# A changed order between attention and the expert blocks: first weights, token rows, ranks and conversions

## The chip, the cores and the metric

One NeuronCore of a Trainium2 chip runs the whole kernel. The metric is the device time of one execution in microseconds (us), median of several runs. The engines are TensorE (PE; its weight loads are PEld), VectorE (DVE), ScalarE (ACT), GpSimd (POOL) and SyncE (SP), which only issues transfers here. Each engine works off its own instructions in order.

## The reference

Three parts follow each other on 2304 tokens of 512 features.

```python
# attention: 4 batches x 8 heads x 576 x 64, window of 128, a slope per head
scores = scale * q @ k.T - slope * rel            # only 0 <= rel < 128
x = softmax(scores) @ v                           # -> [2304, 512]
# top-1 mixture of 8 experts
logits = x @ w_gate + modality_bias[modality_id]
e = argmax(logits); p = softmax(logits)[e]
x = p * (relu(x @ w1[e]) @ w2[e])
# bilinear stage, weights given as 64-bit floats
out = ((x @ m_w1) * (x @ m_w2)) @ m_w3 @ m_wout
```

## The kernel before

**Numbers.** Float32 products are made of three passes: each operand is split into a high half (rounded to the type that TensorE takes, `fp32r`) and a low half (the rest), and `mm3` adds high x high, high x low and low x high. `split` makes the halves: ScalarE writes the high one (L264), VectorE subtracts for the low one (L266). 64-bit weights arrive as pairs of integers, and `to_f32` makes float32 of them in five VectorE instructions (L694, L698, L701, L704, L707), of which the last two write `x`.

**Stages.** (1) Attention in 40 units of two head pairs; 18 tiles of 128 tokens come out. Behind each tile `gate_logits` computes its logits and stores its rows to DRAM (`xz`). (2) For five groups of tiles `route` picks the expert of each token: one-hot rows `hot_b` (L531), running sums `hcum` (L536), two small matmuls that give the ranks `rk` (L540, L543), and from these the positions `pos1_i` (L556). GpSimd then scatters token numbers to `inv2`. (3) `block_table` starts from a matmul that counts the tokens (`cnt`, L574) and gives, in some 40 small VectorE instructions, for each block of 480 token slots its expert `eb_i`, its first row `row_i` (L630) and its first column. The first block has entries of its own (`eb0_i`, `row0_i`), which are there earlier. (4) The expert blocks: `gather_x` loads a block's token numbers (`ids`, on SP) and gathers its rows from `xz` in four groups of 120 (`xb`, indirect transfers that GpSimd issues); `block_transposes` turns a group round on TensorE (`btp`, four transposes) and splits it; `load_w` and `split_w` bring the expert's weights in eight steps per block (`fw`, halves `fwh` and `fwl`); `ffn_step` does the products (`ph`, `py`). (5) The last stage, `bilinear`, with weights `wt` and products `po` at its end.

**Beside attention.** Since the last two matrices are applied one after the other, m_w3 @ m_wout is computed in advance, in 64 steps (`w_step`, three matmuls of 512 columns each into `pw`, eight steps for one row of results, one bank for all, freed by the ScalarE copy at L759). m_w3 comes in 16 pieces of four steps each: `load_w3` loads one, `cvt_w3` converts it, `w3_transposes` transposes it (`w3tp`, four transposes) and splits it (`w3h`, `w3l`). The list `W_STEPS` says how many steps stand in each of the 40 attention units and the six places behind them: 40 steps in all, 34 of them inside the loop over units, six behind it. The last 24 steps (40 to 63, pieces 10 to 15) follow in a loop of their own, behind the table and the first loads. Steps are numbered from 0 and pieces too: piece 9 serves steps 36 to 39, piece 14 steps 56 to 59, piece 15 steps 60 to 63.

**Order.** The code is traced top to bottom, and a planner then orders each engine's instructions by the code's order and by the times that it expects. `high_priority(PRIO)` moves what it encloses forward in that order. `issue_after(ins)` is an edge: whatever the block issues on the engine of `ins` comes behind `ins` there; instructions of other engines are not touched by it. Before the change, only the last group's `route` has high priority, and it stands ahead of the six steps behind the loop.

**Behind w3's last piece.** `run_blocks` splits the first two weight steps behind the halves of piece 15, then transposes the first block's four row groups, then runs the steps, in which weights are split two steps and loaded three steps ahead.

**Memory.** Tiles live in pools, one stack from the left and one from the right of each partition. The pool of the expert blocks (`fp`: weights and, from another stage on, `wt`) lies on the left on top of the constants and a pad of `PAD` bytes, and the pool of the rows (`xp`) above it. Its lower part takes the place of the attention pool, so its first loads wait until that is free.

Of the kernel before, what the change touches and what calls it, by code (L numbers as in the profile page):

```python
# [18 lines left out]
P = 128  # L19
# [4 lines left out]
RU_LAST = 100  # L24
PAD = 32
NB_STATIC = 5
# [20 lines left out]
def kernel(  # L47
# [456 lines left out]
    def route(g, i0, m):  # L504
# [30 lines left out]
        for j in range(i0, i0 + m):  # L535
# [6 lines left out]
        )  # L542
        nc.tensor.matmul(  # L543
            rk[:, :m, :], lhsT=ones_b, rhs=hcum[:, sl, :], start=False, stop=True
# [10 lines left out]
        )  # L555
        nc.vector.tensor_tensor(out=pos1_i[:, sl], in0=mn, in1=rank[:, sl], op=ALU.add)  # L556
        for j in range(i0, i0 + m):
# [6 lines left out]
            tc.add_to_no_dep_group("scatter", sc.ins)  # L564

    def block_table():

# [4 lines left out]

        np_ = pst("A", [P, 6, E], "cnt")
        nc.tensor.matmul(np_[:, 0, :], lhsT=ones_b, rhs=hcum[:, NT, :], start=True, stop=True)  # L574

# [53 lines left out]
        nc.vector.tensor_scalar_mul(eb, eb, float(CAP))  # L629
        nc.vector.tensor_tensor(out=row_i, in0=r0, in1=eb, op=ALU.add)  # L630

# [50 lines left out]

    def to_f32(pool, raw_t, name, x=None):

# [5 lines left out]
        if x is None:  # L690
# [38 lines left out]

    def cvt_w3(i):  # L730
        st_w["x", i] = to_f32(w_p, st_w.pop(("3", i)), f"w3_{i}")

    def w3_transposes(i):
        x = st_w.pop(("x", i))
        h = w_p.tile([P, 4, P], F32R, tag="w3h", name=f"w3h_{i}", bufs=3)
        l = w_p.tile([P, 4, P], F32R, tag="w3l", name=f"w3l_{i}", bufs=3)
        tp = pst("A", [P, 4, P], f"w3tp_{i}")
        for j in range(4):
            nc.tensor.transpose(tp[:, j, :], x[:, j * P : (j + 1) * P], ident)
        split(h, l, tp)  # L740
        st_w["last"] = (last["a"], last["v"])
        st_w["T", i] = (h, l)
# [6 lines left out]
    def w_step(k):  # L749
# [6 lines left out]
        j = g % 4  # L756
        mm3(pw, h[:, j, :], l[:, j, :], woh[:, g, :], wol[:, g, :], g == 0, g == NG - 1)
        if g == NG - 1:
# [111 lines left out]
    for i in range(nu + 2):  # L870
# [36 lines left out]
    assert not w_jobs  # L907
# [86 lines left out]
    def block_transposes(b, u):  # L994
# [8 lines left out]
        for d in range(ND):  # L1003
            nc.tensor.transpose(tp[:, d, :ru], xb[b][u][:ru, d * P : (d + 1) * P], ident[:ru, :ru])
        us = slice(u * ru, (u + 1) * ru)
# [108 lines left out]
    def run_blocks(b0, b1, extra, after=()):  # L1114
        g0, g1 = b0 * NS, b1 * NS
        for g in range(g0, min(g0 + SA, g1)):
            with ExitStack() as st:
                for a in after:
                    st.enter_context(tc.issue_after(a.ins))
                split_w(g)  # L1120
        for u in range(NU):
            block_transposes(b0, u)
        for b in range(b0, b1):
            for s in range(NS):
                g = NS * b + s
                if g + LA < g1:
                    load_w(g + LA)
                if s == 0 and b + 1 < b1:
# [22 lines left out]
    x_p = xstk.enter_context(tc.tile_pool(name="xp", bufs=2))  # L1151
    first_loads(0, NB_STATIC)
# [363 lines left out]
    jobs.setdefault(g_mid + 1, []).append(lambda: load_wt(0, 1))  # L1516
    run_blocks(0, NB_STATIC, jobs, w3_last)
    with tc.tile_pool(name="cp", bufs=2) as c_p:
# [40 lines left out]
```

## Time and profile before

| | us |
|---|---|
| median of 3 runs | 760.69 |
| the three runs | 766.66, 760.69, 759.67 |
| profiled execution | 757.12 |
| its span, first to last instruction | 755.4 |
| TensorE busy | 734.9 |
| VectorE busy | 526.2 |
| ScalarE busy | 347.3 |
| GpSimd busy | 74.9 |

All rows come from the one profiled execution, in us from the start of its span. A row of instructions has its start, its duration, engine, line, operation, output and inputs, shape and count; in brackets stand the idle time just before it on this engine and what ended that. TensorE's matmuls are pipelined: one starts before the end of the last is reported, so the step from start to start is what counts.

### The profile page before, as it was taken

Reading aid. Unit: us, or ns where it says so; the run is one execution under the profiler, and the core shown is the slowest. Engines: PE = TensorE matmul, PEld = TensorE weight load, DVE = VectorE, ACT = ScalarE, POOL = GpSimd, SP = SyncE. Lnnn points to the kernel's source line nnn. Section 1 sums busy time; section 2 is a strip of 40 time slices with the busy share of each in tenths; the row PEclk is TensorE's granted clock in tenths of the full one; section 3 lists DMA queues with packets and bytes.
Section 4 is the critical chain, followed back from the end, with each engine's and each line's share of the span. In section 5 each row is a group of like instructions: output and inputs, shape, how many; then the busy total and the mean of one; then the engine's idle time right before and its main releaser. Section 6 shows DMA issues by size and latency. Waiting matters only on the chain. (4 is left out here: it accounts for less than half of the span.)

```text
span 755.4 us, 12359 instructions
## 1 busy us (share of the span) xinstructions
PE 734.9 (97%) x4335; PEld 631.5 (84%) x4335; DVE 526.2 (70%) x1351; ACT 347.3 (46%) x778; POOL 74.9 (10%) x105
## 2 busy tenths in 40 slices
PE   7899999999999999999999999999999999999996
PEld 5777777787877788888888899999789997899984
DVE  3688888767689469697994347888657775568721
ACT  4787775866842533333343438231632315323221
POOL 5000200201013202030020000000120001100011
PEclk9999999999999999999999999999999999999999
DMA  7999467264136947979698344643226432233011
GB/s 132 325 312 252 109 179 178 67 161 129 44 84 149 253 144 222 293 196 352 180 297 268 132 133 116 209 123 98 77 71 192 123 96 77 67 118 116 1 43 42
DMA packets 126416, 116.29 MB, mean 154 GB/s; under 512 B 69631, under 2 KB 100735, under 8 KB 126344
## 3 DMA queue, kind: packets, MB, share of 16 engines
q1 hardware_dynamic: 122664, 105.91, 48.7%
q0 software_dynamic: 3680, 9.49, 4.0%
q8 instruction: 36, 0.59, 0.4%
q14 instruction: 36, 0.29, 0.1%
HBM read 87.69 MB, written 27.51 MB: 153 GB/s over the span
## 5 line engine op out<-in xcount | busy, mean ns | idle before, releaser
L264 ACT ACTIVATE wth<-wt 128x896 fp32r<-128x896 f32 x48 | 43.0, 946 | 89.6 <-PE pP L1296 89.6
L266 DVE TENSOR_TENSOR fwl<-fw,fwh 128x1024 fp32r<-128x1024 f32 x40 | 48.8, 1225 | 46.3 <-ACT fwh L264 45.8
L397 ACT ACTIVATE p<-p,mn 128x256 f32<-128x256 f32 (+2 forms) x144 | 68.1, 475 | 21.3 <-DVE mn L392 21.0
L264 ACT ACTIVATE fwh<-fw 128x1024 fp32r<-128x1024 f32 x40 | 42.1, 1062 | 76.6 <-PE ph L282 58.9
L281 PE MATMUL ph<-xbh,fwh 128*128 128x480 f32 (+1 forms) x160 | 60.1, 376 | 0.7 <-ACT xbh L264 0.7
L282 PE MATMUL py<-Whl,fwh 128*128 128x480 f32 (+1 forms) x160 | 59.9, 375 | 0.0
L282 PE MATMUL ph<-xbl,fwh 128*128 128x480 f32 (+1 forms) x160 | 59.7, 373 | 0.0
L283 PE MATMUL ph<-xbh,fwl 128*128 128x480 f32 (+1 forms) x160 | 59.6, 373 | 0.0
L283 PE MATMUL py<-Whl,fwl 128*128 128x480 f32 (+1 forms) x160 | 57.8, 373 | 0.0
L281 PE MATMUL po<-Whl,abh 128*128 128x512 f32 x144 | 57.1, 397 | 0.6 <-ACT abh L264 0.6
L283 PE MATMUL po<-Whl,abl 128*128 128x512 f32 x144 | 57.1, 398 | 0.0
L281 PE MATMUL py<-Whl,fwh 128*128 128x480 f32 (+1 forms) x160 | 56.9, 373 | 0.0
L282 PE MATMUL po<-Whl,abh 128*128 128x512 f32 x144 | 56.8, 394 | 0.0
L266 DVE TENSOR_TENSOR abl<-ab,abh 128x512 fp32r<-128x512 f32 x36 | 24.7, 690 | 40.7 <-ACT abh L264 40.6
L266 DVE TENSOR_TENSOR wtl<-wt,wth 128x896 fp32r<-128x896 f32 x48 | 51.8, 1083 | 1.6 <-ACT wth L264 1.4
L392 DVE CUSTOM_DVE_ANT_0 p<-S,bias 128x256 f32<-128x256 f32 (+1 forms) x128 | 43.8, 385 | 12.6 <-PE S L366 12.2
L1305 DVE TENSOR_TENSOR c<-pA,u 128x384 f32<-128x384 f32 x48 | 26.7, 557 | 33.9 <-PE pA L1296 31.7
L264 ACT ACTIVATE abh<-ab 128x512 fp32r<-128x512 f32 x36 | 22.5, 630 | 57.6 <-PE po L282 40.2
L454 PE MATMUL av<-pT,vr 128*64 128x128 f32 (+2 forms) x576 | 47.9, 275 | 0.0
L1401 POOL DMA_INDIRECT out_dram<-o,sid x18 | 21.6, 1200 | 262.9 <-ACT o L1400 262.9
L454 PEld LDWEIGHTS av<-pT,vr 128*64 128x64 f32 (+1 forms) x576 | 32.5, 136 | 11.5 <-issue 5.0
L418 PE MATMUL PT<-ident,p 128*128 128x128 f32 x224 | 41.0, 290 | 0.3
(256 smaller groups left out, 1944.6 us busy)
## 6 DMA issues: line engine op xcount, KB each, us to landing
wt<-wT SPq DMA_DIRECT2D x48, 448.0 KB, 3.3
fw<-in_moe_w_dram SPq DMA_DIRECT2D x40, 512.0 KB, 4.2
raw_w<-in_moe_w_dram SPq DMA_DIRECT2D x16, 512.0 KB, 5.1
raw_m<-in_moe_w_dram SPq DMA_DIRECT2D x32, 256.0 KB, 5.4
wT<-ms SPq DMA_DIRECT2D x16, 448.0 KB, 5.4
yT<-zf SPq DMA_DIRECT2D x20, 256.0 KB, 5.8
x<-yT SPq DMA_DIRECT2D x12, 384.0 KB, 5.5
vr<-in_v_dram SPq DMA_DIRECT2D x16, 256.0 KB, 4.6
```

Of the source, the lines that this page charges most:

```text
L264: last["a"] = nc.scalar.activation(out=hi, in_=src, func=AF.Copy, scale=scale)
L266: last["v"] = nc.vector.tensor_tensor(out=lo, in0=src, in1=f32(hi), op=ALU.subtract)
L281: nc.tensor.matmul(dst, lhsT=lh, rhs=rh, start=start, stop=False)
L282: nc.tensor.matmul(dst, lhsT=lh, rhs=rl, start=False, stop=False)
L283: return nc.tensor.matmul(dst, lhsT=ll, rhs=rh, start=False, stop=stop)
L392: nc.vector.tensor_tensor_reduce(out=p[:, j, t, :nk], in0=s[j][:, t, :nk], in1=bi, scale=1.0, scalar=BIG, op0=ALU.add, op1=ALU.min, accum_ ...
L397: nc.scalar.activation(out=p[:, j, t, :nk], in_=p[:, j, t, :nk], func=AF.Exp, scale=-1.0, bias=m1, accum_out=sm[:, col : col + 1],)
L418: nc.tensor.transpose(pt[:, t, kb, :], p[:, j, t, kb * P : (kb + 1) * P], ident)
L454: nc.tensor.matmul(av[j * D : (j + 1) * D, hp, cs], lhsT=raw["v", b, cc][:n_k, 2 * hp + j, :], rhs=rhs, start=(i_k == 0), stop=(i_k == len ...
L1305: last["d"] = nc.vector.tensor_tensor(out=out, in0=in0, in1=in1, op=op)
L1401: sc = nc.gpsimd.indirect_dma_start(out=out, out_offset=bass.IndirectOffsetOnAxis(ap=sid[g][:, j, 0:1], axis=0), in_=o, in_offset=None, bo ...
```

## The change

- The six steps behind the loop (34 to 39): first the transposes of piece 9, then four steps (12 matmuls), then the last group's `route` on TensorE, the count of tokens right behind its ranks, then the two other steps. `block_table` gets high priority.
- Conversions: the last two instructions of piece 12's, and all of those of pieces 13 to 15, come on VectorE behind the positions of the last group.
- Loads: the first block's ids and two weight steps, then the second block's ids and gathers, then the third weight step.
- When piece 14 has been transposed, the first two weight steps are split, behind the halves of piece 14 and behind `row_i`; the halves of piece 15 come behind these splits.
- The first block's four row groups are transposed behind steps 56, 59, 61 and 62, and the next steps behind them on TensorE. The splits of weight steps 2 and 3 come behind the last group's splits.
- `PAD` goes from 32 to 416 bytes; `wt` halves get tiles of 1024 elements and start 32 elements (128 bytes) into them.

```diff
-PAD = 32
+PAD = 416
+WT_PAD = 32
+RK_STEPS = 2
@@ route: last["rk"] and last["pos"] are kept; block_table: st_w["row"]
+    def count_tokens():
+        st_w["cnt"] = np_ = pst("A", [P, 6, E], "cnt")
+        last["rk"] = nc.tensor.matmul(
+            np_[:, 0, :], lhsT=ones_b, rhs=hcum[:, NT, :], start=True, stop=True
+        )
@@ to_f32(..., behind=None)
-        nc.vector.scalar_tensor_tensor(
-            out=x, in0=low, scalar=2.0**-52, in1=p2.bitcast(F32), op0=ALU.mult, op1=ALU.mult
-        )
-        nc.vector.tensor_tensor(out=x, in0=x, in1=w.bitcast(F32), op=ALU.add)
+        with tc.issue_after(behind.ins) if behind else nullcontext():
+            nc.vector.scalar_tensor_tensor(
+                out=x, in0=low, scalar=2.0**-52, in1=p2.bitcast(F32), op0=ALU.mult, op1=ALU.mult
+            )
+            nc.vector.tensor_tensor(out=x, in0=x, in1=w.bitcast(F32), op=ALU.add)
@@ the places of W_STEPS
-                at(i - LEAD[2], lambda j=j: w3_transposes(j))
+                if ks + 4 < sum(W_STEPS):
+                    at(i - LEAD[2], lambda j=j: w3_transposes(j))
@@ behind the loop over units
-    todo += [lambda: None] * 4
-    for i, f in enumerate(todo):
-        f()
-        for f in w_jobs.pop(nu + 2 + i, []):
+    *todo, route_last = todo
+    w_last = [f for i in sorted(w_jobs) for f in w_jobs.pop(i)]
+    assert not todo
+    w3_transposes(j_in - 1)
+    with ExitStack() as st:
+        st.enter_context(tc.issue_after(st_w["t"].ins))
+        for i, f in enumerate(w_last):
+            if i == len(w_last) - RK_STEPS:
+                with tc.issue_after(st_w["mm"].ins):
+                    route_last()
+                with tc.issue_after(last["rk"].ins):
+                    count_tokens()
+                st.enter_context(tc.issue_after(last["rk"].ins))
             f()
...
-    block_table()
+    with tc.high_priority(PRIO):
+        block_table()
@@ first loads
-    def first_loads(b0, b1):
-        gather_x(b0)
+    def first_loads():
+        gather_x(0)
         with tc.issue_after(last["ids"].ins):
-            for g in range(b0 * NS, min(b0 * NS + LA, b1 * NS)):
+            for g in range(SA):
                 load_w(g)
+        gather_x(1)
+        with tc.issue_after(last["ids"].ins):
+            load_w(SA)
@@ run_blocks
-        for g in range(g0, min(g0 + SA, g1)):
-            with ExitStack() as st:
-                for a in after:
-                    st.enter_context(tc.issue_after(a.ins))
-                split_w(g)
-        for u in range(NU):
-            block_transposes(b0, u)
...
+                        if g < SA:
+                            for i in x_first:
+                                st.enter_context(tc.issue_after(i.ins))
                         split_w(g + SA)
@@ steps 40 to 63
+    X_STEP = [n_w - 8 + i for i in (0, 3, 5, 6)]
+    x_first = []
     for n in range(k_in, n_w):
         j, first = w_piece(n)
-        if first:
+        if first and j < n_j - 1:
             w3_transposes(j)
             if j + 2 < n_j:
                 load_w3(j + 2)
-            if j + 1 < n_j:
-                cvt_w3(j + 1)
-        w_step(n)
-    w3_last = st_w["last"]
+            with tc.issue_after(last["pos"].ins) if j > j_in + 1 else nullcontext():
+                cvt_w3(j + 1, last["pos"] if j > j_in else None)
+        if first and j == n_j - 2:
+            with (
+                tc.issue_after(last["a"].ins),
+                tc.issue_after(last["v"].ins),
+                tc.issue_after(st_w["row"].ins),
+            ):
+                for g in range(SA):
+                    split_w(g)
+            with tc.issue_after(last["wa"].ins), tc.issue_after(last["w"].ins):
+                w3_transposes(j + 1)
+        with ExitStack() as st:
+            if x_first:
+                st.enter_context(tc.issue_after(last["bt"].ins))
+            w_step(n)
+        if n in X_STEP:
+            with tc.issue_after(st_w["mm"].ins):
+                block_transposes(0, X_STEP.index(n))
+            x_first = [last["a"], last["v"]]
@@ split_wt
-            f_p.tile([P, 7, P], F32R, tag=f"w{x}", name=f"wt{x}_{g}_{f}_{k}", bufs=4) for x in "hl"
+            f_p.tile([P, 2 * DM], F32R, tag=f"w{x}", name=f"wt{x}_{g}_{f}_{k}", bufs=4)[
+                :, WT_PAD : WT_PAD + 7 * P
+            ].rearrange("p (s c) -> p s c", s=7)
+            for x in "hl"
```

## Rows read from the trace of the kernel before

**Rows 1.** The page, part 1: TensorE's busy time, share of the span, instructions.

```profile
PE 734.9 (97%) x4335; PEld 631.5 (84%) x4335; DVE 526.2 (70%) x1351; ACT 347.3 (46%) x778; POOL 74.9 (10%) x105
```

**Rows 2.** Windows of the core; first numbers: window, its length, each engine's busy time.

```profile
core 0: us, PE busy (x) PEld busy (x) DVE busy (x) ACT busy (x) POOL busy (x), PEclk, DMA share, GB/s
...
225.00:230.00 5.00, 3.20 (x17) 2.06 (x16) 4.48 (x21) 0.81 (x2) 0.00 (x0) 0.98 0.78 96
230.00:235.00 5.00, 4.70 (x18) 3.44 (x17) 4.49 (x27) 1.58 (x3) 2.41 (x3) 0.68 0.42 95
...
240.00:245.00 5.00, 5.00 (x27) 4.14 (x26) 4.51 (x18) 1.58 (x3) 3.58 (x4) 1.00 1.06 351
...
250.00:255.00 5.00, 4.47 (x23) 3.54 (x22) 4.86 (x5) 3.92 (x6) 1.81 (x2) 1.00 0.57 183
255.00:260.00 5.00, 4.07 (x20) 2.96 (x21) 1.97 (x3) 1.21 (x3) 2.62 (x3) 1.00 1.03 328
...
280.00:300.00 20.00, 20.00 (x99) 17.36 (x99) 18.70 (x45) 7.12 (x10) 4.03 (x4) 1.00 0.78 226
```

**Rows 3.** Waits in 215 to 275 us: total, times, longest.

```profile
PE rk L540 <- DVE hot_b L531: 1.1, 1, 1.1
...
PE pw L281 <- ACT w3h L264: 1.0, 2, 0.7
...
PE btp L1004 <- DVE xbl L266: 0.8, 2, 0.5
...
PE ph L281 <- ACT xbh L264: 0.7, 1, 0.7
```

**Rows 4.** Timeline of TensorE.

```profile
225.60 0.39 PE L283 MATMUL pw<-woh,w3l 128*128 128x512 f32 x1
...
249.04 0.40 PE L281 MATMUL pw<-woh,w3h 128*128 128x512 f32 x1
...
253.58 0.39 PE L283 MATMUL pw<-woh,w3l 128*128 128x512 f32 x1
253.81 0.57 PE L1004 MATMUL btp<-ident,xb 120*128 120x120 f32 x4
...
257.10 0.70 PE L281 MATMUL ph<-xbh,fwh 128*128 128x480 f32 x2 [0.66 <-ACT xbh L264]
```

**Rows 5.** Windows of one tile's instructions: `pw`, then `w3tp`, then `btp`.

```profile
225.90:257.10 31.20, 22.81 (x85) 16.23 (x84) 2.35 (x4) 0.95 0.70 180
...
225.90:257.10 31.20, 3.90 (x28) 3.37 (x28) 4.70 (x7) 3.99 (x7) 0.95 0.70 180
...
225.90:257.10 31.20, 2.41 (x16) 1.76 (x16) 1.98 (x4) 2.29 (x4) 0.95 0.70 180
```

**Rows 6.** Timeline of VectorE.

```profile
226.86 0.17 DVE L531 TENSOR_TENSOR hot_b<-iota_em,mnx 128x16 bf16<-128x16 f32 x1
...
230.58 0.15 DVE L556 TENSOR_TENSOR pos_i<-mnx,rank 128x2 int32<-128x2 f32 x1
...
242.27 0.16 DVE L630 TENSOR_TENSOR row_i<-r,eb 128x12 int32<-128x12 f32 x1
...
248.72 0.69 DVE L266 TENSOR_TENSOR w3l<-w3tp,w3h 128x512 fp32r<-128x512 f32 x1 [4.13 <-ACT w3h L264]
249.66 4.63 DVE L266 TENSOR_TENSOR fwl<-fw,fwh 128x1024 fp32r<-128x1024 f32 x4 [0.25 <-ACT fwh L264]
```

**Rows 7.** Timeline of ScalarE.

```profile
248.57 3.90 ACT L264 ACTIVATE fwh<-fw 128x1024 fp32r<-128x1024 f32 x4
```

**Rows 8.** Transfers issued in 237 to 240 us: count, size, median us to landing.

```profile
fw<-in_moe_w_dram SPq DMA_DIRECT2D x4, 512.0 KB, 4.4
...
xb<-xz,ids POOLq DMA_INDIRECT x1, 7.6
```

**Rows 9.** Timeline of GpSimd.

```profile
239.28 1.15 POOL L981 DMA_INDIRECT xb<-xz,ids  x1 [5.55 <-DMA ids<-inv]
```

**Rows 10.** Timeline of TensorE in the last stage.

```profile
528.02 0.39 PE L281 MATMUL po<-Whl,abh 128*128 128x512 f32 x1
...
529.17 0.40 PE L283 MATMUL po<-Whl,abl 128*128 128x512 f32 x1
```

More of the change, by code (lines that the diff above doesn't have):

```diff
@@ L542, in route @@
         )
-        nc.tensor.matmul(
+        last["rk"] = nc.tensor.matmul(
             rk[:, :m, :], lhsT=ones_b, rhs=hcum[:, sl, :], start=False, stop=True
@@ L555, in route @@
         )
-        nc.vector.tensor_tensor(out=pos1_i[:, sl], in0=mn, in1=rank[:, sl], op=ALU.add)
+        last["pos"] = nc.vector.tensor_tensor(
+            out=pos1_i[:, sl], in0=mn, in1=rank[:, sl], op=ALU.add
+        )
         for j in range(i0, i0 + m):
@@ L564, in route @@
             tc.add_to_no_dep_group("scatter", sc.ins)
+    def count_tokens():
+        st_w["cnt"] = np_ = pst("A", [P, 6, E], "cnt")
+        last["rk"] = nc.tensor.matmul(
+            np_[:, 0, :], lhsT=ones_b, rhs=hcum[:, NT, :], start=True, stop=True
+        )
     def block_table():
@@ L571, in t @@
             return rp.tile([P, *s], F32, tag=nm, name=nm)
-        np_ = pst("A", [P, 6, E], "cnt")
-        nc.tensor.matmul(np_[:, 0, :], lhsT=ones_b, rhs=hcum[:, NT, :], start=True, stop=True)
+        np_ = st_w["cnt"]
         fe, f0 = t("fe", E), t("f0", 1)
@@ L629, in block_table @@
         nc.vector.tensor_scalar_mul(eb, eb, float(CAP))
-        nc.vector.tensor_tensor(out=row_i, in0=r0, in1=eb, op=ALU.add)
+        st_w["row"] = nc.vector.tensor_tensor(out=row_i, in0=r0, in1=eb, op=ALU.add)
         tot, pc, cs = t("tot", E), t("pc", NB_MAX, E), t("cs", NB_MAX)
@@ L681, in load_f64, with to_f32 @@
         return t
-    def to_f32(pool, raw_t, name, x=None):
+    def to_f32(pool, raw_t, name, x=None, behind=None):
         high = raw_t[:, :, 1]
@@ L728, in load_w3, with cvt_w3 @@
         )
-    def cvt_w3(i):
-        st_w["x", i] = to_f32(w_p, st_w.pop(("3", i)), f"w3_{i}")
+    def cvt_w3(i, behind=None):
+        st_w["x", i] = to_f32(w_p, st_w.pop(("3", i)), f"w3_{i}", behind=behind)
     def w3_transposes(i):
@@ L738, in w3_transposes @@
         for j in range(4):
-            nc.tensor.transpose(tp[:, j, :], x[:, j * P : (j + 1) * P], ident)
+            st_w["t"] = nc.tensor.transpose(tp[:, j, :], x[:, j * P : (j + 1) * P], ident)
         split(h, l, tp)
@@ L756, in w_step @@
         j = g % 4
-        mm3(pw, h[:, j, :], l[:, j, :], woh[:, g, :], wol[:, g, :], g == 0, g == NG - 1)
+        st_w["mm"] = mm3(
+            pw, h[:, j, :], l[:, j, :], woh[:, g, :], wol[:, g, :], g == 0, g == NG - 1
+        )
         if g == NG - 1:
@@ L901 @@
             f()
-    todo += [lambda: None] * 4
-    for i, f in enumerate(todo):
-        f()
-        for f in w_jobs.pop(nu + 2 + i, []):
+    *todo, route_last = todo
[11 more added lines that the diff above has]
+                st.enter_context(tc.issue_after(last["rk"].ins))
             f()
-    assert not w_jobs
     if j_in < n_j:
@@ L1003, in block_transposes @@
         for d in range(ND):
-            nc.tensor.transpose(tp[:, d, :ru], xb[b][u][:ru, d * P : (d + 1) * P], ident[:ru, :ru])
+            last["bt"] = nc.tensor.transpose(
+                tp[:, d, :ru], xb[b][u][:ru, d * P : (d + 1) * P], ident[:ru, :ru]
+            )
         us = slice(u * ru, (u + 1) * ru)
@@ L1105, with run_blocks @@
     LA, SA = 3, 2
-    def first_loads(b0, b1):
-        gather_x(b0)
+    def first_loads():
+        gather_x(0)
         with tc.issue_after(last["ids"].ins):
-            for g in range(b0 * NS, min(b0 * NS + LA, b1 * NS)):
+            for g in range(SA):
                 load_w(g)
-    def run_blocks(b0, b1, extra, after=()):
+        gather_x(1)
+        with tc.issue_after(last["ids"].ins):
+            load_w(SA)
+    def run_blocks(b0, b1, extra):
         g0, g1 = b0 * NS, b1 * NS
-        for g in range(g0, min(g0 + SA, g1)):
-            with ExitStack() as st:
-                for a in after:
-                    st.enter_context(tc.issue_after(a.ins))
-                split_w(g)
-        for u in range(NU):
-            block_transposes(b0, u)
         for b in range(b0, b1):
@@ L1127, in run_blocks @@
                     load_w(g + LA)
-                if s == 0 and b + 1 < b1:
+                if s == 0 and b + 1 < b1 and b > 0:
                     gather_x(b + 1)
@@ L1151 @@
     x_p = xstk.enter_context(tc.tile_pool(name="xp", bufs=2))
-    first_loads(0, NB_STATIC)
+    first_loads()
+    X_STEP = [n_w - 8 + i for i in (0, 3, 5, 6)]
+    x_first = []
     for n in range(k_in, n_w):
         j, first = w_piece(n)
-        if first:
+        if first and j < n_j - 1:
             w3_transposes(j)
@@ L1516 @@
     jobs.setdefault(g_mid + 1, []).append(lambda: load_wt(0, 1))
-    run_blocks(0, NB_STATIC, jobs, w3_last)
+    run_blocks(0, NB_STATIC, jobs)
     with tc.tile_pool(name="cp", bufs=2) as c_p:
```

1 line of the change is left out of this document (added).

## The prediction

> **What bounds the kernel now.** I read the page first: TensorE is busy for 97% of the span [rows 1], so only two things can move the time: TensorE standing still, or TensorE running slowly. Then the windows for TensorE's busy time and granted clock [rows 2]. Later windows are full, as 280:300 is; those worth reading lie between 225 and 260 us: TensorE is busy 3.20 of 5 us in 225:230, the clock is 0.68 in 230:235, and 0.53 and 0.93 us are missing in the last two. This is the stretch between attention and the expert blocks, where only the products of w3 with w_out fill TensorE. The waits of this stretch say who was late [rows 3]: the one-hot rows for the last ranks (1.1 us), the high halves of w3's transposed pieces (1.0 us in two waits), and the splits of the first block's rows (0.8 and 0.7 us). That is 3.6 us of standing still.
>
> The clock: 0.68 over 5 us means 3.2 us at the lower of its two levels (1.2 instead of 2.4 GHz), and 0.98 in the window before means 0.2 us more [rows 2]. Of 3.4 us at half speed, 1.7 us are lost. Before it fell, TensorE had stood still twice, for the one-hot rows and for the first of the two high halves.
>
> The ledger of the stretch runs from the product that starts at 225.60 to the first expert matmul at 257.10 [rows 4]. A product of 512 columns takes a step of (253.58 - 249.04)/20 = 0.227 us (20 steps lie between these two rows), so the next one could have started at 225.83, and 31.3 us follow. In them lie 84 matmuls of products (the 85th counted is the one at 225.60), 28 transposes of w3 and 16 of the rows [rows 5]: 84 x 0.227 = 19.1 us; four transposes take 0.57 us with the last one's end hanging over [rows 4], so about 0.11 us each, 44 x 0.11 = 4.8 us; ranks and count some 0.4 us. That is 24.3 us of work. Half clock 1.7 and waits 3.6 make 29.6. The remaining 1.7 us I put down to changeovers between transposes and products, about a dozen at 0.13 us. So **all that this change can win on TensorE in this stretch is 1.7 + 3.6 = 5.3 us**, 0.7% of the time. Behind 257.10 nothing is touched but addresses.
>
> **The change part by part.** *Products ahead of the last ranks.* The ninth piece's transposes (0.45 us) and products 36 and 37 (6 x 0.227 = 1.4 us) come to stand in front of the ranks on TensorE; products 34 and 35 stood there already. TensorE is then busy to 225.83 + 0.45 + 0.13 + 1.4 = 227.8. The one-hot rows are written at 227.03 [rows 6], and two running sums follow, some 0.4 us; so nothing is waited for. The piece's input was converted well before. This removes 1.1 us, and 0.7 of the waits for high halves (the longest in rows 3), because the ninth piece is now transposed products earlier. Both waits stand just before the clock's fall, so I take the fall as gone too: 1.7 us. Sum 3.5 us. Bounds: 0.6 us less if VectorE puts the piece's low half (0.69 us [rows 6]) into the rank chain, so that ranks come that much later; 1.7 less if the clock falls all the same.
>
> *Conversions behind positions, table first.* No work is added; VectorE's order changes. Before, positions are written only at 230.58 [rows 6], 3.6 us after the one-hot rows, because conversions stand between. With these behind, ranks at 227.8 + 0.2 and three dependent steps, an estimated 0.25 us each, give positions at about 228.9, 1.8 us earlier. The table then runs ahead of conversions, so that the first rows of the later blocks (242.27 before) come some microseconds sooner. Behind this queue the conversions of pieces 12 to 15, and behind them w3's last transposes. Before, VectorE had nothing left after the last table steps and waited 4.1 us for the last piece [rows 6]; so a delay of 1 to 2 us, on top of TensorE's gain, still fits. Cost 0; if that cover is gone, TensorE waits for the twelfth or the last piece, 0 to 1.5 us.
>
> *First weights split between the last pieces.* Two of the four splits move from behind the last piece's halves to in front of them. On VectorE that is 2 x 1.16 us (four take 4.63) [rows 6], on ScalarE 2 x 0.98 us (four take 3.90) [rows 7]. They need the first loads, which are issued behind the ids, as these wait for the last scatter, and land 4.4 us later [rows 8]. If the whole line moves with positions, the second load has landed well before the fourteenth piece is transposed: no wait. Behind the splits queue the last piece's halves, the copies of finished product rows on ScalarE and the splits of the token rows. Such a copy frees the single bank of products between products 55 and 56, where transposes covered it before. If a split of 1 us stands ahead of it, TensorE waits. I take 0.3 us, bounds 0 and 1.0.
>
> *Rows' transposes between products.* All four groups now stand behind products 56, 59, 61 and 62, where before three of them stood in a row after the last product. The waits for the rows' splits (0.8 us) and for the first high half (0.7 us) are covered by products of 0.7 us each: minus 1.5 us, with 0.2 us left for the last group. Three more changeovers: plus 0.4 us. The new risk is a wait of TensorE itself: its order is fixed, so a group whose rows have not landed holds the products behind it. Before, positions end at 230.73, the first gather starts at 239.28 [rows 9] and takes 7.6 us to land [rows 8], so the first rows are there at 246.9, 16.1 us behind the positions. With positions at 228.9 that gives 245.0. TensorE reaches this point after 21 products, 24 to 28 transposes, ranks and changeovers, at 225.83 + 14.3 + 2.9 + 0.4 + 1.1 = 244.5. I take a wait of 0.5 us; bounds 0 and 2.4 (positions as before).
>
> *Loads.* On SP the second block's ids go ahead of the third weight load, with a read of the table in front of them. Behind that read waits the third load, which is first needed two steps into the blocks, some 10 us later. The second block's gathers wait on POOL until the first block's rows are transposed, as before, and nothing else stands behind them there. Cost 0.
>
> *Addresses.* The pad shifts the blocks' weights and rows by 384 bytes; the last stage's weights are put back to where they were, modulo 512. No instruction is added. Can it move a matmul's step? Products of the same 512 columns step at 0.227 us in this stretch and at (529.17 - 528.02)/5 = 0.230 us in the last stage [rows 4, 10], with their operands elsewhere. So the nearest rows give 3 ns either way, on 960 + 1008 + 432 = 2400 matmuls (block loops, bilinear products, output products): plus or minus 7.2 us. I take 0, since the two rows lie so close. The Trainium skill, "SBUF — State Buffer", section "SBUF: two separate sides", says that TensorE has its own port there and never waits for another engine; by it the term is exactly 0. The 3 ns between like products neither bear that out nor refute it.
>
> **Sum.** 3.5 + 1.5 - 0.2 - 0.4 - 0.3 - 0.5 = 3.6 us; the second wait for a high half, 0.3 us, stays. The profiled execution took 757.12, 1.7 more than its span of 755.4, and should come to 753.5. The median of the runs, 760.69, lies 3.6 above it, so the forecast there is **757.1 us**.
>
> **The rivals.** *The rows come too late.* If positions gain nothing, the rows land at 246.9, TensorE stands for 2.4 us instead of 0.5, and 1.9 of the 3.6 us go: 759.0. For it: the DMA engines' busy share is 1.06 in 240:245 [rows 2], and scatter, ids and gather wait for each other in line. Against: positions no longer wait for conversions.
>
> *VectorE or ScalarE becomes late, and the clock falls once more.* The splits ahead of the last piece cost 1.0 us instead of 0.3, and a stretch of transposes and waits brings the 1.7 us back: 759.5. Against it: from 253.8 to 257.1 TensorE ran only transposes and stood still between them, and the clock stayed at 1.00 in 255:260 [rows 2, 4]. The Trainium skill, "TensorE: Matmul & The Clock Gate", section "Part 4: PE-mode transpose", says that transposes do not count as busy in the same way; by it this is a stretch behind which the clock should fall, and the trace shows one behind which it did not.
>
> *It doesn't do what it says.* Within an engine, the order that no edge fixes is a planner's. If the rank chain on VectorE moves back as far as TensorE's products move forward, ranks are still waited for, and the gain is about 0.5 us: 760.2.
>
> *Slower: the addresses.* If the shifted operands step 3 ns slower, 7.2 us are added and 3.6 taken away: 764.3. It decides from 3.6/2400 = 1.5 ns per matmul on. For it speaks only the difference of the two rows; against it, that the operands of one matmul lie far apart in memory with or without the shift. The same the other way gives 749.9.
>
> **How the numbers follow.** Forecast 0.52; rows late 0.18; late engines and clock 0.12; not as it says 0.06; addresses slower 0.05, faster 0.04; 0.03 for what I don't see. The range holds the first four with the bounds of their terms: from all of the 5.3 us and 2.5 us for the scatter of runs, 752.9, to no gain at all, 761. A measurement of this kernel tells 1% (7.6 us) from no change; its three runs lie 7 us apart. More than 1% faster needs the addresses: 0.05. More than 1% slower needs over 4.7 ns per matmul, or something unseen: 0.04. Within 1%: 0.91.
>
> **What would show it.** Right: in the changed profile the windows after the ranks have the clock at 1.00, there is no wait for one-hot rows, positions are written near 229, the rows land near 245 and the first expert matmul starts near 253.5. Wrong: a wait of the rows' transposes for a gather of over 1 us; a second fall of the clock; a wait for the last piece's halves; or another step of the matmuls in the later stages.

## The result and the profile after

The changed kernel is faster by less than 1%: **757.59 us** (15 runs, 751.56 to 762.27) against 763.45 for the kernel before (15 runs, 759.67 to 767.12). The ratio is 0.9915, 95% interval 0.9889 to 0.9941, or 6.5 us. The forecast was 757.1 us, worked out as a gain of 3.6 us; the gain was larger, and its parts were not those of the prediction.

The profiled execution took 751.56 us, 1.8 more than its span of 749.8. Of the 5.6 us between the two profiles, 4.1 lie in the stretch between attention and the expert blocks, 0.6 in the expert blocks and 1.5 in the last stage; attention ended 0.8 us later. The profiled executions differ by up to 9 us in when attention ends (its last gate group starts between 223.0 and 232.2), whatever the kernel. So stretches of the profile say more here than spans. I measure the stretch from the start of the last gate group (`xlg`) to the first expert matmul: 223.04 to 257.10 before, 34.06 us; after, 223.81 to 253.73, **29.92 us**.

Windows of the changed kernel, with the columns of [rows 2], to be read against them:

```profile
225.00:230.00 5.00, 5.00 (x28) 3.91 (x27) 4.02 (x28) 0.70 (x2) 0.39 (x1) 1.00 0.58 114
230.00:235.00 5.00, 3.94 (x20) 2.88 (x19) 5.00 (x17) 1.57 (x3) 2.89 (x3) 1.00 0.57 108
235.00:240.00 5.00, 4.76 (x25) 3.78 (x24) 5.00 (x16) 1.68 (x3) 0.81 (x1) 1.00 0.18 36
240.00:245.00 5.00, 5.00 (x26) 4.10 (x25) 4.62 (x20) 1.75 (x3) 3.87 (x4) 1.00 0.98 301
245.00:250.00 5.00, 4.70 (x28) 3.71 (x27) 3.86 (x8) 2.29 (x4) 0.99 (x1) 1.00 0.80 232
250.00:255.00 5.00, 5.00 (x27) 3.62 (x26) 2.32 (x4) 3.03 (x5) 2.94 (x3) 1.00 1.01 310
255.00:260.00 5.00, 5.00 (x25) 4.34 (x24) 2.68 (x3) 2.33 (x4) 0.00 (x0) 1.00 1.04 263
```

The clock is 1.00 throughout, and TensorE is full at the ranks and at the end; about 1 us is missing in 230:235. The waits of TensorE in this stretch answer to [rows 3]:

```profile
PE pw L285 <- DVE w3l L268: 0.8, 1, 0.8
...
PE pw L283 <- ACT wraw L771: 0.5, 2, 0.3
...
PE pw L283 <- ACT w3h L266: 0.3, 1, 0.3
```

The waits for one-hot rows and for the splits of the first block's rows are gone. A new one stands at the top, for a low half of w3 from VectorE; the copies of product rows on ScalarE cost 0.5. The timelines of TensorE, VectorE and GpSimd, one after the other, answer to [rows 4, 6, 9]:

```profile
247.07 0.57 PE L1028 MATMUL btp<-ident,xb 120*128 120x120 f32 x4
249.57 0.57 PE L1028 MATMUL btp<-ident,xb 120*128 120x120 f32 x4
251.38 0.57 PE L1028 MATMUL btp<-ident,xb 120*128 120x120 f32 x4
252.50 0.57 PE L1028 MATMUL btp<-ident,xb 120*128 120x120 f32 x4
...
253.73 0.70 PE L283 MATMUL ph<-xbh,fwh 128*128 128x480 f32 x2
```

```profile
227.50 0.18 DVE L533 TENSOR_TENSOR hot_b<-iota_em,mnx 128x16 bf16<-128x16 f32 x1
...
229.18 0.15 DVE L558 TENSOR_TENSOR pos_i<-mnx,rank 128x2 int32<-128x2 f32 x1
...
244.49 0.16 DVE L639 TENSOR_TENSOR row_i<-r,eb 128x12 int32<-128x12 f32 x1
```

```profile
239.19 1.41 POOL L1005 DMA_INDIRECT xb<-xz,ids  x1 [5.99 <-DMA ids<-inv]
```

The last figures are of the transfers issued in 239.1 to 240.8 (median us to landing):

```profile
xb<-xz,ids POOLq DMA_INDIRECT x1, 5.0
```

The four row groups stand between products, none with a wait in brackets. Positions are written at 229.18 (forecast near 229), the first rows land at 239.19 + 5.0 = 244.2 (245.0), the first expert matmul starts at 253.73 (253.5). Only `row_i` went the wrong way: 244.49 where before had 242.27. And the first gather starts no sooner than before's (239.28), though positions are 1.4 us earlier: what brings the rows sooner is its landing, 5.0 us instead of 7.6. SyncE's wait for the last scatter, ahead of the ids, had grown. Before, then after:

```profile
SPq L975 <- DMA inv<-tg,pos_i: 3.7, 1, 3.7
```

```profile
SPq L999 <- DMA inv<-tg,pos_i: 4.9, 1, 4.9
```

The last stage changed as well. In one group of it, 24 output products follow each other with nothing between. First and last of them, before and then after:

```profile
540.28 0.39 PE L281 MATMUL po<-Whl,abh 128*128 128x512 f32 x1
...
545.62 0.40 PE L283 MATMUL po<-Whl,abl 128*128 128x512 f32 x1
```

```profile
536.28 0.40 PE L283 MATMUL po<-Whl,abh 128*128 128x512 f32 x1
...
541.53 0.39 PE L285 MATMUL po<-Whl,abl 128*128 128x512 f32 x1
```

The step is 5.34/23 = 232.2 ns before and 5.25/23 = 228.3 ns after, with the same instructions. By the same reckoning over 41 unbroken second products of the expert blocks (`py`) of 480 columns, 218.2 ns became 216.0, and over 71 of 400 columns, 180.1 became 183.4. The first products (`ph`) of 480 columns did not change: groups of 33 to 35 in a row step at 216.5 to 217.4 ns before and 216.5 to 217.1 after. Where 480 and 400 columns are spoken of below, `py` is meant.

### The profile page after: what moved, and what is told of

It reads as the page before. It is cut to its first block, busy times and chain, and to the rows that moved or that the text cites. A ratio compares the mean times of both kernels' runs of the same rounds, so it can differ in the third digit from the quotient of the medians.

```text
span 749.8 us, 12359 instructions
## 1 busy us (share of the span) xinstructions
PE 728.8 (97%) x4335; PEld 627.9 (84%) x4335; DVE 526.0 (70%) x1351; ACT 347.3 (46%) x778; POOL 77.6 (10%) x105
## 5 line engine op out<-in xcount | busy, mean ns | idle before, releaser
L394 DVE CUSTOM_DVE_ANT_0 p<-S,bias 128x256 f32<-128x256 f32 (+1 forms) x128 | 43.8, 384 | 11.8 <-PE S L368 11.5
```

The costliest lines, as they stand in the source:

```text
L394: nc.vector.tensor_tensor_reduce(out=p[:, j, t, :nk], in0=s[j][:, t, :nk], in1=bi, scale=1.0, scalar=BIG, op0=ALU.add, op1=ALU.min, accum_ ...
```

## The experiments

Runs 7, 10 and 11 were executed once each and serve for the steps of products alone; the others were timed over five rounds beside the kernel before. The stretch is from each run's own profiled execution, one for each kernel, between the rows named above.

| run | ratio, 95% interval | stretch, us |
|---|---|---|
| before | | 34.06 |
| the change | 0.9915 (0.9889 to 0.9941) | 29.92 |
| 1 order without addresses | 0.9928 (0.9891 to 0.9965) | 29.92 |
| 2 addresses alone | 0.9965 (0.9926 to 1.0003) | 34.06 |
| 3 ranks alone | 1.0036 (0.9998 to 1.0075) | 34.91 |
| 4 rows' part alone | 0.9927 (0.9890 to 0.9964) | 32.16 |
| 5 change without conversions | 0.9992 (0.9963 to 1.0021) | 35.06 |
| 6 ranks and conversions | 1.0032 (0.9988 to 1.0075) | 35.32 |
| 8 low halves first | 0.9950 (0.9921 to 0.9980) | 29.77 |
| 9 change, loads as before | 0.9947 (0.9910 to 0.9985) | 34.11 |
| 12 ranks, conversions, loads | 1.0005 (0.9973 to 1.0036) | 32.92 |

**Order and addresses apart (1 and 2).** The changed kernel with before's two numbers, and the kernel before with the change's:

```
-PAD = 416
-WT_PAD = 32
+PAD = 32
+WT_PAD = 0
```

> The changed order with the old addresses (pad 32, last stage's weights at the start of their tiles). Two theories on the 6 us. First, order and addresses both count: the stretch from the last logits product (the row of four that starts at 223.04 before and 223.81 after) to the first expert matmul takes 29.9 us as in the changed kernel (34.1 before), while the expert blocks take 205.2 us and the last stage 285.2 us as before (204.6 and 283.6 after); output products step at 0.231 us; ratio 0.9945. Second, order alone counts and the shorter later stages are chance of one execution: stages in any mixture, ratio 0.9915.

> The kernel before with the pad of 416 bytes and the last stage's weights 128 bytes into their tiles. If addresses count: expert blocks 204.6 us instead of 205.2, last stage 283.6 instead of 285.2, output products at 0.227 us instead of 0.231, py matmuls at 0.216 instead of 0.218, stretch near 34.1 with the fall of the clock; ratio 0.997. If they don't: 205.2, 285.2, ratio 1.000.

The order alone has the whole gain in the stretch, 4.14 us, and its steps are before's: 232.2 ns for output products, 218.2 for 480 columns. The addresses alone leave the stretch as it was and have the changed kernel's steps. So the two do not touch each other. Run 2 shows one thing more. Its order in the stretch is nearly that of before, but its clock did not fall there, and the stretch is 34.06 us all the same. Its waits of TensorE:

```profile
PE btp L1005 <- DVE xbl L267: 1.2, 1, 1.2
PE pw L284 <- DVE w3l L267: 1.1, 1, 1.1
PE rk L541 <- DVE hot_b L532: 1.1, 1, 1.1
PE pw L282 <- ACT w3h L265: 1.0, 2, 0.7
PE ph L282 <- ACT xbh L265: 0.7, 1, 0.7
```

These are 5.1 us, against the 3.6 us and a half clock of 1.7 in before: where TensorE keeps its clock, it comes to VectorE's low half of w3 (`w3l`, 1.1 us) and to the row splits (1.2 instead of 0.8) too early. That is read from one execution of either kind.

**Ranks alone (3).** Products ahead of the last ranks, with the conversions where they stood:

```
+    w3_transposes(j_in - 1)
...
+            if i == len(w_last) - RK_STEPS:
+                with tc.issue_after(st_w["mm"].ins):
+                    route_last()
```

> The kernel before with the one part that puts piece 9's transposes and four steps ahead of the last ranks; conversions, table, loads, splits, rows' transposes and addresses as before. My theory, that this part alone removes the wait for the one-hot rows (1.1 us), the wait for piece 9's high half (0.7 us) and the fall of the clock (1.7 us): stretch about 31.0 us instead of 34.1, ratio 0.996. Rival, that it needs the conversions behind the positions: ranks still waited for, stretch over 33, ratio 0.999.

My theory fell and the rival held. Waits, VectorE's row for the one-hot rows, and windows of TensorE:

```profile
PE rk L542 <- DVE hot_b L533: 3.2, 1, 3.2
```

```profile
235.12 0.17 DVE L533 TENSOR_TENSOR hot_b<-iota_em,mnx 128x16 bf16<-128x16 f32 x1
```

```profile
230.00:235.00 5.00, 2.14 (x9) 1.15 (x7) 3.55 (x14) 0.21 (x1) 0.00 (x0) 1.00 0.95 165
235.00:240.00 5.00, 4.58 (x19) 3.33 (x19) 4.27 (x29) 1.78 (x3) 2.03 (x3) 0.72 0.12 18
```

The last gate group started at 227.12 here, so the one-hot rows come 8.0 us behind it instead of 3.8 before (223.04 to 226.86). Conversions had moved in front of them on VectorE, and with these a wait of 1.45 us for a load of w3. TensorE stood for 3.2 us, and the clock fell behind that.

**Rows' part alone (4).** First splits, order of loads and rows' transposes of the change; ranks, conversions, table and addresses of before.

```
+        if n in X_STEP:
+            with tc.issue_after(st_w["mm"].ins):
+                block_transposes(0, X_STEP.index(n))
```

> The kernel before with the other part: first two weight steps split between the last pieces, second block's ids early, rows' transposes behind steps 56, 59, 61 and 62; ranks, conversions, table and addresses as before. My theory: the waits for the rows' splits go and changeovers come, stretch about 33.0 us instead of 34.1, with the fall of the clock unchanged, ratio 0.9985. Rival, that rows land too late without earlier positions: TensorE stands over 1 us in front of a group, stretch 34 or more, ratio 1.000 or above.

The stretch is 1.90 us shorter: the waits for row splits are gone (1.2 and 0.7 us in run 2), and those for one-hot rows (1.1), high halves (1.0) and the low half (1.1) are as in run 2, at clock 1.00. The timed gain, 2.7 us or more by its interval, is larger than the profile explains.

**The change without the conversions held back (5).**

```
-            with tc.issue_after(last["pos"].ins) if j > j_in + 1 else nullcontext():
-                cvt_w3(j + 1, last["pos"] if j > j_in else None)
+            cvt_w3(j + 1)
```

> The changed kernel with the conversions of w3's pieces not held behind the positions; all else as in the change. First theory (from the run with products ahead of the ranks alone): the conversions are what makes the new place of the ranks pay. Without them held back, VectorE comes to the last one-hot rows about 2 to 3 us later, TensorE stands still for the ranks by 2 to 3 us, the clock falls to half behind it (1.7 us), positions are written near 232 instead of 229, and the rows land near 247 instead of 244.2, just in time or up to 1 us late. Stretch from the last gate group to the first expert matmul 33 to 35 us instead of 29.9; time near before's less 2 us for the addresses, ratio 0.995 to 1.000. Rival, as the prediction had it: the order of VectorE costs nothing on TensorE beyond the positions; ranks waited for by under 1 us, clock 1.00, stretch 30 to 31, ratio 0.992 to 0.994.

The first theory holds, at its upper end. Its wait and windows:

```profile
PE rk L542 <- DVE hot_b L533: 3.6, 1, 3.6
```

```profile
235.00:240.00 5.00, 1.78 (x7) 0.86 (x5) 3.16 (x13) 0.22 (x1) 0.00 (x0) 0.98 1.06 155
240.00:245.00 5.00, 4.56 (x16) 3.65 (x17) 3.03 (x25) 0.94 (x2) 2.11 (x3) 0.50 0.08 18
245.00:250.00 5.00, 5.00 (x23) 3.68 (x22) 5.00 (x15) 0.84 (x2) 0.12 (x1) 0.84 0.10 6
```

A clock of 0.98, 0.50 and 0.84 over 5 us each is 0.2 + 5.0 + 1.6 = 6.8 us at the lower level, so 3.4 us lost. With the wait that is 7.0; other waits of 1.4 us went, and the stretch is 5.1 us longer, 0.5 less than that sum. Without the edit that was costed at nothing, none of the order's gain is left.

**Ranks and conversions, without the rows' part (6).** The edit of run 3 and the one that run 5 leaves out, put on before.

> The kernel before with products ahead of the last ranks and the conversions held behind the positions; rows' transposes, first splits, loads and addresses as before. First theory: the parts take different waits and the clock's fall is taken by either of them, so it is counted once. Then this part alone gives the 3.5 us that the prediction put down to it (1.1 one-hot rows, 0.7 first high half, 1.7 clock): stretch 34.1 less 3.5, 30.6 us, with the waits of the rows' splits (0.8 and 0.7 us) still there, ratio 0.995. Rival: the parts add up. The run with the rows' part alone had 1.9 us less, the whole has 4.1, so this one has 2.2 less: stretch 31.8, ratio 0.997, with the clock falling once in it or another wait in place of the ones removed.

Neither: it is slower than either expected. Positions came as early as in the change (5.4 us behind the last gate group), but now TensorE reached the first row group before its rows. Its timeline and its windows:

```profile
252.27 1.03 PE L1027 MATMUL btp<-ident,xb 120*128 120x120 f32 x4 [2.43 <-issue]
```

```profile
250.00:255.00 5.00, 2.73 (x9) 2.38 (x10) 4.19 (x4) 3.36 (x5) 0.00 (x0) 0.72 1.09 250
255.00:260.00 5.00, 5.00 (x24) 4.06 (x23) 1.79 (x2) 1.57 (x3) 0.99 (x1) 0.94 1.03 347
```

A releaser is not named ("issue"), but the first rows finished landing at 252.1, just ahead of this row. They came 19.0 us behind the start of the positions' row, where before needed 16.3 (the prediction's 16.1 counts from that row's end) and the change 15.0. Two things make these up. From positions to the gather's start it is 8.7 us in before, 10.0 in the change and 11.6 here, where SyncE waited 6.1 us for the last scatter; the gather's landing takes 7.6, 5.0 and 7.4 us. With the change's landing the rows would have been there at 249.7, when TensorE asked for them at 249.8. This is the prediction's rival "the rows come too late", in a partial kernel.

**Which edit lets the rows come in time (9 and 12).** First, the change with the loads as before:

```
-            for g in range(SA):
+            for g in range(LA):
                 load_w(g)
-        gather_x(1)
-        with tc.issue_after(last["ids"].ins):
-            load_w(SA)
...
-                if s == 0 and b + 1 < b1 and b > 0:
+                if s == 0 and b + 1 < b1:
```

> The changed kernel with SyncE's order of loads as before: first block's ids, all first weight loads, and only behind them the ids of the second block. The question is why the ranks and conversions alone lost 1 us while the whole change wins 4. First theory: the gathers wait beside the weight loads; with two more loads in front, the first rows land 2 us or more later behind the positions (about 17 us instead of 15.0), TensorE, whose order puts the first row group in among the products, waits for them by up to 1 us, and the stretch is 30.5 or more instead of 29.9. Rival: the loads cost the rows nothing that TensorE feels, because the first row group stands so late in TensorE's order (2.9 us behind the landing of its rows); then it was the place of the rows' transposes that the ranks needed: stretch 29.9 within 0.3, no wait for rows, clock 1.00, ratio as for the whole change, 0.991 to 0.994.

The first theory holds, and more. TensorE's first row group, GpSimd's first gather, and windows:

```profile
257.21 1.03 PE L1028 MATMUL btp<-ident,xb 120*128 120x120 f32 x4 [2.44 <-issue]
```

```profile
248.14 1.15 POOL L1005 DMA_INDIRECT xb<-xz,ids  x1 [5.79 <-DMA ids<-inv]
```

```profile
255.00:260.00 5.00, 2.79 (x9) 2.43 (x10) 1.49 (x5) 0.57 (x1) 0.00 (x0) 0.69 1.07 243
260.00:265.00 5.00, 5.00 (x28) 4.11 (x28) 1.32 (x2) 1.42 (x3) 0.99 (x1) 0.97 0.94 304
```

The row group starts 9.07 us behind its gather's issue, which in the change lands after 5.0. Run 1 is the closer comparison, since its gather starts as far behind the positions (11.4 us) as here (11.5). With the change's loads it landed after 5.0 us too, and TensorE did not wait:

```profile
247.73 1.00 POOL L1005 DMA_INDIRECT xb<-xz,ids  x1 [6.27 <-DMA ids<-inv]
```

```profile
xb<-xz,ids POOLq DMA_INDIRECT x1, 5.0
```

The wait of 2.44 us and 3.4 us at half clock (1.7 lost) are 4.1 us: the stretch is 4.19 us longer than in the change, all that the order had won there. Second, run 6 with the change's loads added:

> The run with ranks and conversions alone, with the change's order of loads added (two first weight loads beside the first block's gathers, the second block's ids ahead of the third); rows' transposes, first splits and addresses as before. First theory: in that run the rows came too late because four weight loads moved beside the gathers, and the clock's fall followed from TensorE's wait for them. With two loads fewer the rows land about 15 us behind the positions instead of 19, the wait of 2.4 us and the fall (1.7 us) go, and the waits of the rows' splits (1.0 and 0.7 us) stay: stretch 30.9 instead of 35.0, ratio about 0.995. Rival: TensorE still comes to the row group before its rows, because without the rows' transposes placed further back in its order it asks for them too early: a wait of 1 us or more and the clock's fall stay, stretch 33 to 34.5, ratio 0.999 to 1.002.

The wait for rows is gone, as the first theory says; its number is not reached. The wait moved to the row splits, and the clock fell behind it:

```profile
PE btp L1027 <- DVE xbl L268: 2.5, 1, 2.5
```

```profile
260.00:265.00 5.00, 1.87 (x7) 1.23 (x7) 3.33 (x5) 2.65 (x5) 3.46 (x3) 0.78 1.02 322
265.00:270.00 5.00, 5.00 (x15) 4.17 (x15) 0.00 (x0) 0.34 (x1) 0.00 (x0) 0.53 1.02 290
```

On VectorE these row splits queue behind the splits of the third and the fourth weight, of which the last starts at 260.70 and which wait for loads that the new order issues later (from 253.30 on). In the change the row splits stand ahead of these, and the row groups between products. Most of the clock's fall lies behind the first expert matmul: the expert blocks are 2.7 us longer than in before.

**Low halves first (8).** A try at the change's own largest wait:

```
-            with tc.issue_after(last["pos"].ins) if j > j_in + 1 else nullcontext():
+            with tc.issue_after(st_w["v", j_in + 1].ins) if j > j_in + 1 else nullcontext():
```

> The changed kernel with the conversions of pieces 13 to 15 held behind the low half of piece 11 instead of behind the positions. First theory: the wait for a low half of piece 10 (0.76 us) is there because steps of later conversions stand ahead of it on VectorE; with these behind, the low half is written some 0.8 us earlier, the wait is gone, and nothing else gets late, as VectorE had time left at the last piece: stretch 29.9 less 0.7, 29.2 us, ratio to before 0.991, the clock at 1.00 throughout. Rival: the conversions of pieces 13 to 15 come later by as much, their transposes wait, and the wait of 0.7 us only moves there: stretch 29.9 or up to 0.5 more.

The wait of 0.8 us went, as expected, and no other wait of that size came; yet the stretch is only 0.15 us shorter, and the ratio cannot be told from the change's. The profile names waits of 0.6 us in all, 1.0 less than in the change. The other 0.85 us stand in four of TensorE's steps, each 0.16 to 0.26 us longer than its like: one into the transposes of a w3 piece (476 ns instead of 231), and three around the first two row groups (390, 419 and 494 ns instead of about 230). What held these steps the profile does not name. So the rival was right in kind: most of the wait moved behind, in parts too short to be listed. No version here is measurably better than the change.

**Where the step comes from (7, 10, 11).** Three versions of the changed kernel with other numbers: the last weights' shift taken out (7), a pad of 160 bytes (10) and of 288 (11), the last two with the last weights put back.

> The changed kernel with the last stage's weights shifted by 384 bytes too (their own 128 byte shift back is taken out); no instruction or order differs. First theory: a product's step goes by where its operands lie within 512 bytes. The output products of the last stage, 232.3 ns before and 228.5 after, come out at another value again, 230 ns or more (up to 0.2% of the time), the 480 column products stay at 216.1 and the 400 column products at 183.3. Rival: what made the output products faster is the shift of their other operand, and the weights' place does nothing: 228.5 again, and no other row differs.

> The changed kernel with a pad of 160 bytes instead of 416 and the last stage's weights put back to the same place modulo 512 as before. Only addresses differ. First theory (from the run with the weights unshifted): the step of the bilinear products goes by the place of the last stage's weights, so it stays 173.3 ns; the other three steps go by the pad, and lie between or at the values seen: output products 228.5 to 232.3, 480 columns 216.1 to 218.2, 400 columns 180.1 to 183.3. Rival: any pad other than 32 gives the same as 416, because it is the one place of before that is special: 228.5, 216.1, 183.3.

> The changed kernel with a pad of 288 bytes and the last stage's weights put back to the same place modulo 512. As for the pad of 160: first theory, three steps differ from those at 416 and at 32 in their own ways and the bilinear products stay at 173.3 ns; rival, 228.5, 216.1 and 183.3 ns as at 416. A pad at which the 400 column products are back at 180 ns and the others stay at the lower value would win another 0.3 us.

The same 24 output products as above, first and last, with the pad of 160 and then of 288:

```profile
540.69 0.40 PE L283 MATMUL po<-Whl,abh 128*128 128x512 f32 x1
...
545.94 0.39 PE L285 MATMUL po<-Whl,abl 128*128 128x512 f32 x1
```

```profile
545.83 0.39 PE L283 MATMUL po<-Whl,abh 128*128 128x512 f32 x1
...
551.17 0.40 PE L285 MATMUL po<-Whl,abl 128*128 128x512 f32 x1
```

5.25/23 = 228.3 ns at 160, as at 416; 5.34/23 = 232.2 ns at 288, as at 32. The 480 column products go the same way (216.0 and 218.2 ns), the 400 column products the other way (183.4 and 180.1). So there are two values, not one for each place: they change with 128 bytes and come back with 256. Neither theory had this: at 160 the numbers of both came out, at 288 both failed, but for the bilinear products, which the first theory had staying at 173.3 ns. In run 7 the output products stayed at 228.3 ns, as the rival had it; but the bilinear products moved, which neither had. Here are the first and the last of the same 60, in the change and then in run 7:

```profile
465.40 0.33 PE L1345 MATMUL pV<-x2l,wth 128*128 128x384 f32 x1
...
475.62 0.43 PE L1345 MATMUL pS<-x2h,wth 128*128 128x384 f32 x1
```

```profile
465.18 0.34 PE L1345 MATMUL pV<-x2l,wth 128*128 128x384 f32 x1
...
475.60 0.38 PE L1345 MATMUL pS<-x2h,wth 128*128 128x384 f32 x1
```

That is 10.22/59 = 173.2 ns against 10.42/59 = 176.6: the last weights' shift back keeps these products fast. The shifts move what other engines write and read in these tiles, too; so the runs show that places matter, and not whether it is the product's own reading or a meeting with other accesses.

## Why the prediction came out as it did

The time fell inside the range because the ledger of the order was right: waits and clock of one stretch, 5.3 us, of which 4.14 were won. That it came within 0.5 us of 757.1 is luck. The gain was 6.5 us where 3.6 were forecast, more than the 5.3 that the prediction took for all there was to win, because the addresses gave what it had put at nothing; and the kernel before, 760.69 in the three runs that the forecast was counted from, came out at 763.45. From 760.69 the measured ratio gives 754.2, still in the range. The windows, waits and landmarks named for a right forecast came, but so did one of the signs named for a wrong one: another step of the matmuls in the later stages. Step by step:

- **Addresses: taken as 0, measured at 2.2 us faster.** This is the term of the sum that was mis-sized most. 432 output products x 3.9 ns = 1.7 us, 384 `py` products of 480 columns x 2.2 = 0.8, less 96 of 400 columns x 3.3 = 0.3; the expert blocks and the last stage did get 0.6 and 1.5 us shorter. The two rows that I judged by were too few: five steps of output products, at the start of the stage, take 230 ns in before, and 24 unbroken ones show 232.2. The bounds of 3 ns were of the right size, the choice of 0 within them was not. The Trainium skill, "SBUF — State Buffer", section "SBUF: two separate sides", gives TensorE its own port; the prediction read from it that a shift costs exactly nothing. The runs show another step with the same instructions on every engine and only places moved, so that reading doesn't hold.
- **Products ahead of the last ranks: 3.5 us.** The one-hot rows' 1.1 and 0.7 of the high halves came as forecast. The half clock's 1.7 was probably wrong in kind. Run 2 had no fall and the same stretch; part of what the clock gives back seems to become a wait for VectorE's low half, 1.1 us there and 0.76 in the change. The step counted the fall as a cost by itself, which two executions, one with the fall and one without, do not bear out.
- **Conversions behind positions: cost 0.** No wait shows a cost of it, but its weight was wrong: the ranks' 3.5 us rest on it. The prediction took the one-hot rows' time (227.03) from before as given; with ranks moved alone they come 4 us later relative to attention (run 3), and without this edit the change is no faster than before (run 5).
- **Table first.** `row_i` came later, not sooner: 20.7 us behind the start of the last gate group, against 19.2 in before. In runs 6 and 12, which leave the table's priority out, it stands 20.7 us behind as well; so nothing in the runs shows an effect of that edit.
- **Loads: 0.** Wrong: with before's loads the stretch loses 4.2 us (run 9). I looked at who needs the third load later, and not at what it delays: the gathers beside it. The first one landed after 7.0 to about 9 us with before's loads (before, runs 3, 6 and 9) and after 5.0 with the change's (the change, runs 1 and 4). And the 16.1 us from positions to rows did not move along with positions: SyncE's wait for the last scatter grew from 3.7 us to 4.9 in the change and 6.1 to 6.3 in runs 1, 6 and 9, so that with before's loads rows came 19.0 and 20.4 us behind the positions (runs 6 and 9). That they landed near the 245.0 forecast was luck: of the 1.4 us by which the positions were earlier, the scatter took back 1.2, and the shorter landing, which the prediction had not counted on, made up for that.
- **Rows' transposes: -1.5, first splits +0.3, wait for rows +0.5.** Rows' part alone, 1.9 us (run 4), is the waits for row splits of run 2. The bank's copies cost 0.5 instead of 0.3. No wait for rows came: they landed 0.8 us earlier than forecast, and above all TensorE reached the first group at 247.07, 2.6 us later than the 244.5 of the prediction, which had left out attention's end (0.8 us later here) and the waits ahead of this point (1.6 us).
- **Sum of the order: 3.6 forecast, 4.14 measured.** By waits: 3.6 + 1.7 before, 1.6 after, so 3.7 us; 0.4 more I can't place row by row. I had 0.4 for more changeovers on the other side.

The parts don't add up. Alone, ranks are +0.9 us, ranks with conversions +1.3, with the loads -1.1 (with 2.7 us given back behind it), and rows' part, which has the loads too, -1.9; all of them -4.1. Each edit moves TensorE's wait to the next supplier: one-hot rows, then the gathered rows, then their splits. In runs 3, 5, 6, 9 and 12 TensorE stood for over 2 us at one of these, and the clock fell behind it.

One thing stays open: why the clock fell in before, behind waits of 1.1 us and less, and not in runs 2 and 4 with the same waits. The Trainium skill, "TensorE: Matmul & The Clock Gate", section "Part 4: PE-mode transpose", says that transposes don't count as busy in the same way. In run 12 the clock did fall among row transposes, which it did not in before [rows 2, 4]; but TensorE stood for 2.5 us there, so the runs can't tell transposes from standing still.

## What to carry to other kernels

When an engine's work is moved ahead, ask of each thing that it will then meet whether its time in the old profile was set by a supplier with room to spare, or by a queue that moves as well; cost the edits as a chain, since one that "costs nothing" may be what the others rest on. A fall of the clock beside waits need not be a cost of its own: the stretch was 34.06 us with it and without it, as the waits were longer without. And when addresses shift, take a long unbroken group of like products as the row for the step.

## What the hardware showed that I had not expected

- The step of a product depends on the place of its operands: 128 bytes of shift move it from 232.2 to 228.3 ns (512 columns), 218.2 to 216.0 (`py`, 480), 180.1 to 183.4 (`py`, 400) and 173.2 to 176.6 (384), and 256 bytes bring the old value back for the first three. Not every product gains from the same place, and `ph` shows no change.
- A gather that landed 5.0 us after its issue with two 512 KB loads issued just ahead of it (the change, runs 1 and 4) needed 7.0 to about 9 us with four issued around it (before, runs 3, 6 and 9).
